# Where the scales of v are made: moving v's maxima, the store and load of its scales, and the first tile's attention-v inside a fused attention kernel

## The chip, the cores and the metric

The kernel runs on one core of a Trainium2 chip. The metric is the device time of one execution in microseconds (us); several executions are timed and their median is given. One further execution was taken with the hardware profiler, and all rows below come from it.

The engines are named as the profile names them: PE is TensorE's matmul side and PEld its weight load, DVE is VectorE, ACT is ScalarE, POOL is GpSimd, and SPq is SyncE's queue, from which this kernel issues every DMA.

## The reference, cut to what matters

```python
scores = scale * np.matmul(q, k.transpose(0, 1, 3, 2))      # 4 batches, 12 heads, 448 x 448
scores = np.einsum('bhij,hg->bgij', scores, w_pre)          # heads mixed
scores = scores - np.max(scores, axis=-1, keepdims=True)
attn = np.exp(scores)
attn = attn / (np.sum(attn, axis=-1, keepdims=True) + 1e-09)
attn = np.einsum('bhij,hg->bgij', attn, w_post)             # heads mixed again
attn_out = np.matmul(attn, v)
x = attn_out as [batch, 448, 768]
x = x + gated MLP of x (w_in, layer norm, token mixing w_sg, w_out)
x = two rotated token mixings and a channel matmul (w_theta, w_tok_r, w_tok_i, w_ch)
```

Only the attention part is touched by the change. It takes roughly the first 475 us of the span.

## The kernel before, in words

**Tiles and blocks.** The 448 query rows of a batch are cut into four tiles of 120, 120, 120 and 88 rows. Because heads are mixed, the scores of a tile (`s`, rows by heads by columns) are laid out again so that ten query rows times twelve heads fill 120 partitions: such a group of ten rows is a *block* (`blk`). A batch has 12 + 12 + 12 + 9 = 45 blocks, the last of a batch has only eight rows (96 partitions), and there are 180 blocks in all.

**Steps.** The function `attention` builds one long program: a loop over a step number s, from -7 to 191. In each step every engine gets its share for several blocks at different stages:

- SyncE: `relayout` of block s+7 (L217, a DMA from `s` to `blk`; five buffers, so block r waits until block r-5 has been used), and after it whatever the table `early` holds for the step
- TensorE: `premix` of block s+4 (L223, into `psB`, two buffers), matmuls for scores of a later tile (L203) and attention-v (L329) where the table `work` has them, then `postmix` of block s (L277, L278, L280)
- VectorE: `rowmax` of block s+4 (L229), `at_lo` of block s-1 (L308), the reciprocal for block s+2 (L250), `p_lo` of block s+1 (L262)
- ScalarE: the exponential of block s+3 (L236), `at_hi` of block s-1 (L302), copies of scores out of PSUM (L209, L207)
- GpSimd: `p_hi` of block s+2 (L255) and the small operation before the reciprocal (L244)
- after these, on whichever engine, what the table `late` holds for the step.

Each engine runs its own list in the order written. SyncE, too, issues its DMAs one after another: a DMA that has to wait holds all that are behind it. Since `premix` of block s+4 belongs to step s, the start of the `premix` of a block tells in which step TensorE is: block 44 is step 40. Its row is easy to find, since it alone in its batch has 96 partitions.

**The v path.** v is kept as two half-precision parts with a power-of-two scale per column. For a batch, three loads of v transposed (`vT`, L133, 448 KB each, two buffers) and three reductions (`v_max`, L148) give the maxima `vmx`. `v_scale` makes the scales `sv` and their inverses in six short VectorE operations (L87 to L156). `v_scale_out` (L162) stores the 768 scales to DRAM (`vs_d`), as 128 partitions of six single values. `v_scale_in` (L166) loads them back into all partitions (`vbc`); it waits until the store has ended. Then, for each of six pairs of heads, v is loaded (`vraw`, L173), multiplied (`v_mul`, GpSimd, L178), rounded (`v_hi`, ScalarE, L181) and its rest taken (`v_lo`, GpSimd, L185, three steps after `v_mul`).

**What sets the place of these.** The tables are filled by `put(table, step, function, arguments)`. `put_v(b, s, m, gap)` places `v_scale` of batch b late in step s, its store and load some steps after, and `v_mul` of the six pairs from step m on, `gap` steps apart. For the first batch it is called with steps of its own, for the other three with `first[b, 0] - VA[b]`, where `first[b, 0]` is the batch's first block (45, 90, 135). `DD[t][c]` says how many steps after the last block of tile t of any batch the attention-v of pair c is put.

Of the kernel before, what the change touches and what calls it, by code (L numbers as in the profile page):

```python
# [23 lines left out]
LD, LB, LE, LH, LL, EB, PB, SB = LDS  # L24
QO = 3
WARM = 16
VA = (0, 7, 7, 7)
VB = (0, 2, 3, 4)
XO = 1
DD = ((3, 5, 7, 9, 11, 13), (3, 4, 5, 6, 7, 8), (3, 4, 5, 6, 8, 10), (3, 4, 5, 6, 7, 8))  # L30
TX = 1
EX0 = 3
EX1 = 18
VM = 5
EXP_BITS = 0x7F800000


def attention(tc, nc, io, xT, B, extra, tail):
# [17 lines left out]
    with ExitStack() as es:  # L56
# [304 lines left out]
        early, work, late = {}, {}, {}  # L361

        def put(d, s, fn, *a):
            d.setdefault(s, []).append((fn, a))
# [6 lines left out]
        def unit(T, c):  # L371
            lo, hi = win[T]
            return lo + (c * (hi - lo)) // NP

        def put_v(b, s, m, gap):
            put(late, s, v_scale, b)
            put(early, s + 2, v_scale_out, b)
            put(early, s + 5, v_scale_in, b)
            for c in range(NP):
                put(early, m - 2, load_v, b, c)  # L380
                put(late, m, v_mul, b, c)
                put(late, m + 2, v_hi, b, c)
                put(late, m + 3, v_lo, b, c)
                m += gap

        for T in range(2, nt):
            b, t = tiles[T]
            for c in range(NP):
                put(work, unit(T, c), scores, b, t, c)
            put(early, win[T][0] - QO, load_q, b, t)  # L390
            if t == 0:
                for c in range(NP):
                    put(early, unit(T - 1, c), load_k, b, c)
                for c in range(0, NP, 2):
                    s = unit(T - 1, c)
                    put(early, s, load_vT, b, c)
                    put(late, s + 3, v_max, b, c)
                put_v(b, first[b, 0] - VA[b], first[b, 0] + VB[b], 3)
        for T in range(nt):
            b, t = tiles[T]  # L400
            l = last[tiles[T]]
            for c in range(NP):
                s = l + DD[t][c]
                put(work, s, attn_v, b, t, c)
# [26 lines left out]
            scores(0, 0, c)  # L431
        consts()
        for c in range(0, NP, 2):
            put(early, -LD + c // 2, load_vT, 0, c)
            put(late, -LD + 1 + c // 2, v_max, 0, c)
        put_v(0, -LD + 4, VM, 2)
        for s in range(-LD, NB + 12):
            if s == -LD:
                for fn, a in early.get(s - 1, []):
# [736 lines left out]
def build(tc, nc, io, out):  # L1176
    with tc.manual_schedule(), ExitStack() as top:
        dram = top.enter_context(tc.tile_pool(name="scratch", bufs=1, space=bass.MemoryType.DRAM))
        xT = dram.tile([DM, B * S], F32, name="xT")
        x2T = dram.tile([DM, B * S], F32, name="x2T")  # L1180
        d = Dense(tc, nc, io, xT, x2T, out)
        d.scratch(dram)
        right, left1, left2 = ExitStack(), ExitStack(), ExitStack()
        tail, win_es, last_u, end = moe1(d, left1, right)
        th_es = moe2(d, left2, win_es, last_u, left1)
        for i in range(4):
            tail.setdefault(-2 + 2 * i, []).append(d.step)
        jobs = d.decode_all(io["w_in"], HF, DFF, d.win_d)
        jobs += d.decode_all(io["w_in"], 0, HF, d.win_d, 128 * KE)
        attention(tc, nc, io, xT, B, jobs, tail)  # L1190
        while d.at < len(d.units):
            d.step()
        th_es.close()
        right.close()
        left2.close()
# [54 lines left out]
```

## Time and profile before

| | us |
|---|---|
| median of 3 runs | 1044.81 |
| lowest and highest | 1042.14 and 1047.06 |
| the profiled execution's own time | 1047.47 |
| span of the profiled execution | 1045.6 |
| PE busy, share of the span | 982.3, 94% |
| DVE, POOL, ACT busy | 775.5, 622.4, 586.6 |

The profiled execution lies 2.66 us above the median; 1.87 us of its time lie outside the span. A busy share is an average over the whole span and says nothing about one stage. What a stage is bound by is read from what ended the idle time of TensorE there, and from the chain of waits.

### The profile page before, as it was taken

How to read it: one execution, taken by the hardware profiler on the slowest of the kernel's cores; microseconds unless marked ns; L12 is line 12 of the kernel's file. 1: busy time of each engine (PE TensorE's matmuls, PEld its weight loads, DVE VectorE, ACT ScalarE, POOL GpSimd, SP SyncE). 2: the span in 40 equal slices, each digit the busy share in tenths (PEclk: the TensorE clock that was granted, in tenths of full speed). 3: DMA queues.
4: the chain of work that ended last, by engine and by line, in shares of the span. 5: the costliest groups of instructions: out<-in, count | busy, mean ns of one | idle time of the engine just before them, and what ended most of it. 6: DMA issues, size and time to landing. Idle time of an engine off the chain costs nothing.

```text
span 1045.6 us, 21830 instructions
## 1 busy us (share of the span) xinstructions
PE 982.3 (94%) x7848; PEld 742.7 (71%) x7848; DVE 775.5 (74%) x1458; ACT 586.6 (56%) x1374; POOL 622.4 (60%) x818
## 2 busy tenths in 40 slices
PE   7789999999999999997978999799999999999998
PEld 2445655565656555566756979587888999999997
DVE  2799878987888878985989998898896724925611
ACT  4577778786777778775754645454364412613310
POOL 0596558754686548854656877775666643753622
PEclk9899999999999999998989999999999999999999
DMA  5757565556556564347353676758956131130021
GB/s 191 154 167 221 142 139 183 180 168 129 161 193 203 131 158 152 131 108 265 113 155 89 213 225 199 229 188 274 335 184 226 41 106 31 32 106 16 31 76 53
DMA packets 135504, 159.47 MB, mean 153 GB/s; under 512 B 30309, under 2 KB 120933, under 8 KB 135397
## 3 DMA queue, kind: packets, MB, share of 16 engines
q1 hardware_dynamic: 135397, 158.08, 50.3%
q8 instruction: 63, 1.03, 0.4%
q14 instruction: 44, 0.36, 0.1%
HBM read 86.66 MB, written 32.85 MB: 114 GB/s over the span
## 4 chain that ended last, share of the span: by engine, by line
PE 57%; DVE 20%; DMA 9%; POOL 5%; issue 4%; ACT 3%; SPq 1%; DVEq 0%; ACTq 0%; POOLq 0%
PE ps L564 27%; PE psB L223 10%; PE psA L203 5%; PE psD L329 5%; DVE da L604 3%; PE psC L280 3%; PE psC L277 3%; DMA blk<-s 2%; PE psC L278 2%; DVE pl L262 2%; DVE da L602 2%; DVE dp L610 2%; DMA xres<-xT 2%; DVE dp L618 2%; DMA xraw<-xT 1%
## 5 line engine op out<-in xcount | busy, mean ns | idle before, releaser
L255 POOL TENSOR_SCALAR ph<-e,rc 120x448 f16<-120x448 f32 x180 | 163.9, 911 | 147.3 <-DVE rc L250 99.8
L223 PE MATMUL psB<-blk,kpre 120*120 120x448 f32 x360 | 177.3, 575 | 13.0 <-DMA blk<-s 8.2
L229 DVE TENSOR_REDUCE nmx<-psB 120x1 f32<-120x448 f32 x180 | 111.3, 618 | 49.9 <-PE psB L223 40.8
L262 DVE SCALAR_TENSOR_TENSOR pl<-e,rc,ph 120x448 f16<-120x448 f32 x180 | 147.4, 819 | 0.0
L236 ACT ACTIVATE e<-psB,nmx 120x448 f32<-120x448 f32 x180 | 114.3, 635 | 43.1 <-DVE nmx L229 43.0
L308 DVE SCALAR_TENSOR_TENSOR al<-psC,ah 128x480 f16<-128x480 f32 x180 | 116.1, 645 | 8.2 <-ACT ah L302 7.9
L277 PE MATMUL psC<-wh,ph 120*128 120x120 f16 x720 | 97.7, 218 | 10.9 <-DVE al L308 7.1
L302 ACT ACTIVATE ah<-psC 128x480 f16<-128x480 f32 x180 | 103.0, 572 | 7.6 <-PE psC L280 4.9
L209 ACT ACTIVATE s<-psA 120x896 f32<-120x896 f32 (+1 forms) x90 | 82.5, 917 | 42.5 <-PE psA L203 41.1
L564 PE MATMUL ps<-wtok,z 128*128 128x448 f32 x504 | 104.8, 368 | 0.4 <-POOL z L560 0.4
L564 PEld LDWEIGHTS ps<-wtok,z 128*128 128x128 f32 x504 | 94.4, 188 | 10.1 <-POOL z L560 0.8
L277 PEld LDWEIGHTS <-ph 120*128 120x128 f16 x720 | 68.8, 99 | 44.3 <-issue 18.6
L278 PE MATMUL psC<-wl,ph 120*128 120x120 f16 x720 | 97.1, 218 | 2.4 <-issue 2.4
L329 PEld LDWEIGHTS <-ah 128*128 128x128 f16 x1536 | 76.6, 99 | 31.2 <-issue 31.2
L203 PE MATMUL psA<-k,q 64*120 64x448 f32 (+1 forms) x384 | 96.2, 580 | 1.0 <-ACT s L209 1.0
L564 PE MATMUL ps<-wth,x2s 128*128 128x384 f32 x504 | 92.5, 338 | 2.0 <-POOL x2s L560 2.0
L564 PE MATMUL ps<-u,wch 128*128 128x448 f32 x432 | 89.9, 368 | 0.0
L564 PEld LDWEIGHTS ps<-wth,x2s 128*128 128x128 f32 x504 | 87.2, 188 | 2.8 <-POOL x2s L560 2.6
L560 POOL TENSOR_TENSOR z<-zz,z 128x384 fp32r<-128x384 f32 x56 | 61.9, 1125 | 45.8 <-ACT z L557 45.8
L564 PEld LDWEIGHTS ps<-u,wch 128*128 128x128 f32 x432 | 81.0, 188 | 8.1
L278 PEld LDWEIGHTS <-ph 120*128 120x128 f16 x720 | 71.2, 99 | 14.4 <-issue 14.2
L329 PE MATMUL psD<-vl,ah 128*128 128x64 f16 x768 | 78.0, 194 | 1.1 <-POOL vl L185 1.1
(124 smaller groups left out, 2171.9 us busy)
## 6 DMA issues: line engine op xcount, KB each, us to landing
blk<-s SPq DMA_DIRECT2D x176, 210.0 KB
draw<-in_w_in SPq DMA_DIRECT2D x24, 256.0 KB
vraw<-in_vN SPq DMA_DIRECT2D x24, 256.0 KB
k<-in_kvT SPq DMA_DIRECT2D x24, 224.0 KB
vT<-in_kvT SPq DMA_DIRECT2D x12, 448.0 KB
xraw<-xT SPq DMA_DIRECT2D x24, 224.0 KB
xres<-xT SPq DMA_DIRECT2D x24, 224.0 KB
x2T<-xres SPq DMA_DIRECT2D x24, 224.0 KB
```

Source lines behind the costliest of these rows:

```text
L203: nc.tensor.matmul(ps[e][:n, :S], q[p, o:o + n], k[p], start=True, stop=True)
L223: nc.tensor.matmul(ps[:r, :S], kpre[:r, :r], sblk.pop(s)[:r], start=True, stop=True)
L229: nc.vector.tensor_reduce(out=m[:r], in_=mix[s][:r, :S], axis=AX.X, op=ALU.max, negate=True)
L236: nc.scalar.activation(out=e[:r], in_=mix.pop(s)[:r, :S], func=AF.Exp, bias=nmx.pop(s)[:r], accum_out=sm[:r])
L255: nc.gpsimd.tensor_scalar(out=p[:r], in0=ex[s][0][:r], scalar1=rec[s][:r], scalar2=0.0, op0=ALU.mult, op1=ALU.add)
L262: nc.vector.scalar_tensor_tensor(out=p[:r], in0=ex.pop(s)[0][:r], scalar=rec.pop(s)[:r], in1=ph[s][:r], op0=ALU.mult, op1=ALU.subtract)
L277: nc.tensor.matmul(ps[:, jc, :, :n], cols(a, jc), wh[:r, :, :n], start=(jc == 0), stop=False)
L278: nc.tensor.matmul(ps[:, jc, :, :n], cols(a, jc), wl[:r, :, :n], start=False, stop=False)
L302: nc.scalar.activation(out=at_view(s, at[b, t][0]), in_=src, func=AF.Copy, scale=2.0 ** -17)
L308: nc.vector.scalar_tensor_tensor(out=al, in0=src, scalar=2.0 ** -17, in1=ah, op0=ALU.mult, op1=ALU.subtract)
L329: nc.tensor.matmul(ps[:, o:o + 64], a[:, i0:i0 + 128], v[:, jc, 64 * e:64 * e + 64], start=(o == 0 and m == 0), stop=(o == 320 and m == le ...
L564: self.nc.tensor.matmul(ps, l, r, start=(i == 0), stop=(i == len(terms) - 1))
```

## The change

It moves instructions; none is added or taken away. For the first batch the loads of `vT` move from steps -7, -6, -5 to steps -5, -4, -3, the three `v_max` from late in steps -6, -5, -4 to late in steps -2, -1, 0, `v_scale` from step -3 to step 1, and the first `v_mul` from step 5 to step 10 (two steps apart as before). For the other batches `v_scale` moves from seven to eleven blocks ahead of the batch. In all batches the store of the scales stands one step after `v_scale` instead of two, and their load eight steps after it instead of five, so that seven steps lie between store and load where there were three. `DD[0]` holds for the first tile of every batch: its attention-v moves from 3, 5, 7, 9, 11, 13 to 6, 7, 9, 10, 12, 13 steps after the tile's last block.

```diff
-VA = (0, 7, 7, 7)
+VA = (0, 11, 11, 11)
 VB = (0, 2, 3, 4)
-DD = ((3, 5, 7, 9, 11, 13), (3, 4, 5, 6, 7, 8), (3, 4, 5, 6, 8, 10), (3, 4, 5, 6, 7, 8))
+DD = ((6, 7, 9, 10, 12, 13), (3, 4, 5, 6, 7, 8), (3, 4, 5, 6, 8, 10), (3, 4, 5, 6, 7, 8))
-VM = 5
+VM = 10
...
         def put_v(b, s, m, gap):
             put(late, s, v_scale, b)
-            put(early, s + 2, v_scale_out, b)
-            put(early, s + 5, v_scale_in, b)
+            put(early, s + 1, v_scale_out, b)
+            put(early, s + 8, v_scale_in, b)
...
         for c in range(0, NP, 2):
-            put(early, -LD + c // 2, load_vT, 0, c)
-            put(late, -LD + 1 + c // 2, v_max, 0, c)
-        put_v(0, -LD + 4, VM, 2)
+            put(early, -LD + 2 + c // 2, load_vT, 0, c)
+            put(late, -2 + c // 2, v_max, 0, c)
+        put_v(0, 1, VM, 2)
```

SyncE at the start of the program, from the first block on (L217 is a block's relayout, L133 a load of v transposed, L162 the store of the scales, L166 their load). Before:

```order
L217 DMA blk<-s 120x1x448
L133 DMA vT<-in_kvT 128x2x448
L217 DMA blk<-s 120x1x448
L133 DMA vT<-in_kvT 128x2x448
L217 DMA blk<-s 120x1x448
L133 DMA vT<-in_kvT 128x2x448
L217 DMA blk<-s 120x1x448 x4
L162 DMA vs_d<-sv 128x6x1
L217 DMA blk<-s 120x1x448 x2
L588 DMA draw<-in_w_in 128x512
L217 DMA blk<-s 120x1x448
L166 DMA vbc<-vs_d 128x768
```

And now:

```order
L217 DMA blk<-s 120x1x448 x3
L133 DMA vT<-in_kvT 128x2x448
L217 DMA blk<-s 120x1x448
L133 DMA vT<-in_kvT 128x2x448
L217 DMA blk<-s 120x1x448
L133 DMA vT<-in_kvT 128x2x448
L217 DMA blk<-s 120x1x448 x4
L588 DMA draw<-in_w_in 128x512
L217 DMA blk<-s 120x1x448
L162 DMA vs_d<-sv 128x6x1
L217 DMA blk<-s 120x1x448 x2
L138 DMA q<-in_qT 128x720
```

The third load of v stood ahead of block 3 and stands ahead of block 5; the store stood ahead of block 7 and stands ahead of block 10.

SyncE ahead of the second batch (the row with 96 is block 44, the last of the first batch). Before:

```order
L217 DMA blk<-s 96x1x448
L138 DMA q<-in_qT 128x720
L217 DMA blk<-s 120x1x448 x3
L162 DMA vs_d<-sv 128x6x1
L217 DMA blk<-s 120x1x448 x2
L358 DMA xT<-x 128x3x120
```

And now:

```order
L358 DMA xT<-x 128x3x120
L217 DMA blk<-s 120x1x448 x2
L162 DMA vs_d<-sv 128x6x1
L588 DMA draw<-in_w_in 128x512
L217 DMA blk<-s 120x1x448
L217 DMA blk<-s 96x1x448
L138 DMA q<-in_qT 128x720
```

The store stood behind block 47 and ahead of block 48; it stands behind block 42 and ahead of block 43. In the third and fourth batch it moves in the same way, with no load of weights (`draw`) right behind it.

VectorE at the start, from its first reductions on (L148 is a maximum of v, L229 a row maximum, L87 the first operation of `v_scale`). Before:

```order
L148 TENSOR_REDUCE vmx<-vT 128x2 x2
L229 TENSOR_REDUCE nmx<-psB 120x1
L148 TENSOR_REDUCE vmx<-vT 128x2
L229 TENSOR_REDUCE nmx<-psB 120x1
L87 TENSOR_SCALAR vmx<-vmx 128x6
```

And now:

```order
L229 TENSOR_REDUCE nmx<-psB 120x1 x3
L250 RECIPROCAL rc<-rc 120x1
L148 TENSOR_REDUCE vmx<-vT 128x2
L229 TENSOR_REDUCE nmx<-psB 120x1
L250 RECIPROCAL rc<-rc 120x1
L262 SCALAR_TENSOR_TENSOR pl<-e,rc,ph 120x448
L148 TENSOR_REDUCE vmx<-vT 128x2
```

The first maximum of v stood ahead of the row maximum of block 0 and stands behind that of block 2.

## Rows read from the trace of the kernel before

**Rows 1.** The page: busy us, share of the span and instructions of each engine.

```profile
PE 982.3 (94%) x7848; PEld 742.7 (71%) x7848; DVE 775.5 (74%) x1458; ACT 586.6 (56%) x1374; POOL 622.4 (60%) x818
```

**Rows 2.** Chain of waits, first 200 us: start us, us, what the end waited on.

```profile
19.80 1.10 DVE vmx L148
20.91 3.46 DMA vT<-in_kvT
24.40 1.09 DVE vmx L148
...
27.23 11.20 DMA blk<-s
...
132.21 10.66 DMA blk<-s
```

**Rows 3.** Timeline of PE, premix of blocks 0, 5, 7, 10, 12, 43: [idle before <-releaser].

```profile
17.88 0.98 PE L223 MATMUL psB<-blk,kpre 120*120 120x448 f32 x2 [1.10 <-DMA blk<-s]
...
29.81 0.97 PE L223 MATMUL psB<-blk,kpre 120*120 120x448 f32 x2
...
38.57 1.82 PE L223 MATMUL psB<-blk,kpre 120*120 120x448 f32 x2 [5.38 <-DMA blk<-s]
...
45.83 0.97 PE L223 MATMUL psB<-blk,kpre 120*120 120x448 f32 x2
...
50.38 0.97 PE L223 MATMUL psB<-blk,kpre 120*120 120x448 f32 x2
...
128.82 0.97 PE L223 MATMUL psB<-blk,kpre 120*120 120x448 f32 x2
```

**Rows 4.** Timeline of SyncE's queue: the stores of the scales, and what followed.

```profile
26.74 0.38 SPq L162 DMA_DIRECT2D vs_d<-sv  x1
27.23 1.69 SPq L217 DMA_DIRECT2D blk<-s  x2
...
36.90 0.35 SPq L166 DMA_DIRECT2D vbc<-vs_d  x1
...
131.72 0.39 SPq L162 DMA_DIRECT2D vs_d<-sv  x1
...
363.53 0.39 SPq L162 DMA_DIRECT2D vs_d<-sv  x1
```

**Rows 5.** Timeline of DVE: row maxima of two neighbouring steps, and two p_lo.

```profile
30.91 0.62 DVE L229 TENSOR_REDUCE nmx<-psB 120x1 f32<-120x448 f32 x1
...
32.66 0.62 DVE L229 TENSOR_REDUCE nmx<-psB 120x1 f32<-120x448 f32 x1
...
119.97 0.67 DVE L262 SCALAR_TENSOR_TENSOR pl<-e,rc,ph 120x448 f16<-120x448 f32 x1
...
361.89 0.67 DVE L262 SCALAR_TENSOR_TENSOR pl<-e,rc,ph 120x448 f16<-120x448 f32 x1
```

**Rows 6.** Busy us by stretch: length, PE, PEld, DVE, ACT, POOL, PEclk, DMA share, GB/s.

```profile
140.00:150.00 10.00, 9.04 (x104) 5.08 (x104) 6.90 (x15) 6.30 (x16) 4.59 (x10) 1.00 0.81 200
190.00:200.00 10.00, 9.39 (x84) 5.56 (x85) 8.80 (x18) 7.15 (x19) 8.17 (x11) 0.83 0.44 145
250.00:260.00 10.00, 7.82 (x72) 3.93 (x70) 5.03 (x13) 5.43 (x15) 3.36 (x6) 1.00 0.58 84
370.00:380.00 10.00, 8.02 (x86) 4.52 (x84) 5.97 (x14) 5.80 (x14) 5.18 (x9) 1.00 0.56 135
```

**Rows 7.** The same in stretches of 2 us, the first and last with a lowered clock.

```profile
36.00:38.00 2.00, 0.00 (x0) 0.00 (x0) 0.00 (x0) 0.00 (x0) 0.00 (x0) 0.95 0.70 110
...
44.00:46.00 2.00, 2.00 (x19) 1.49 (x18) 1.86 (x6) 1.45 (x4) 1.23 (x2) 0.84 0.82 221
```

**Rows 8.** Timeline of PE: two more waits.

```profile
190.61 0.21 PE L277 MATMUL psC<-wh,ph 120*128 120x120 f16 x1 [2.05 <-DVE rc L250]
...
441.97 0.19 PE L329 MATMUL psD<-vl,ah 128*128 128x64 f16 x1 [1.06 <-POOL vl L185]
```

**Rows 9.** Chain of waits, 360 to 378 us: a piece in which PE waited for nothing shown.

```profile
371.40 1.64 issue
```

## The prediction

> **What bounds the kernel now.** I read the page's busy shares first: TensorE is busy for 94% of the span [rows 1], so nearly every idle stretch of TensorE inside attention is a loss, and what another engine saves is worth nothing unless TensorE was waiting for it. Then I read the chain of waits over the first 200 us [rows 2], which is where all first uses of the v path lie. It shows two kinds of loss. At the start VectorE reduces v before it may take row maxima: the chain runs through the maxima at 19.80 and 24.40 and through a load of v of 3.46 us between them. And twice it runs through a block's relayout that lasted 11.20 and 10.66 us. Then I read SyncE's timeline [rows 4]: both of these blocks were issued right behind a store of the scales (26.74 and 131.72). The store itself is small but slow: the load that waits for it follows at 36.90, 10.2 us after it. So a store of the scales holds up everything behind it in the DMA engines for some 11 us: a block issued behind it lands 11.7 us (27.23 + 11.20 - 26.74) or 11.15 us (132.21 + 10.66 - 131.72) after the store's issue. What that costs depends on one thing alone: how much work TensorE still has ahead when the store is issued.
>
> In the first batch it had too little: the premix of block 7 stood for 5.38 us [rows 3], and the granted clock fell to half (1.2 of 2.4 GHz), from 0.95 in 36 to 38 us to 0.84 in 44 to 46 us [rows 7], which is 0.2 us, three whole stretches and 0.64 us at half clock, 6.8 us in all. In the second batch TensorE's idle time in the ten microseconds of the landing is 0.96 us, in the third 2.18 us and in the fourth 1.98 us [rows 6], together 5.1 us. So in the later batches the store is nearly hidden now.
>
> **The change part by part.**
>
> *First batch, up to block 5.* Row maxima no longer stand behind the loads of v, so blocks 0 to 4 go through earlier. But the third load of v needs the buffer of the first, and so waits for the first maximum, which now stands behind the row maximum of block 2; on SyncE block 5 is queued behind that load, and TensorE waits for block 5. Following it by hand: the premix of block 0 starts at 17.88 and takes 0.98 [rows 3]; two more premixes and two groups of score matmuls of about that length bring block 2 to about 22.8, its row maximum to 23.4, the maximum of v (1.10 us [rows 2]) to 24.5; load and block are issued by 25.0. The load of v landed 3.46 us after its issue; I give block 5 that much at least, and a microsecond more for standing behind the load. So its premix starts at 28.5 to 29.5 instead of 29.81 [rows 3]. Nearly all of the gain ends in this new wait: 0.3 to 1.3 us are left.
>
> *First batch, the store.* v_scale now comes after p_lo of step 1 on VectorE. With the premix of block 5 (0.97) from 28.5 to 29.5 on, then its row maximum, at_lo, reciprocal and p_lo (a step takes VectorE 1.75 us, 32.66 - 30.91 [rows 5]) and the first operations of v_scale, about 1.0 us, the store goes out at 32.2 to 33.2, and block 10, right behind it, lands 11.7 us later, at 43.9 to 44.9; take 44.2. TensorE wants block 10 after three more steps of VectorE, at about 39. So the hole is there again, of some 5 us, and ends 1.6 us earlier than block 10 had its turn (45.83 [rows 3]). The half clock comes again too, but later: it lay on steps 3 to 5 (38.57 to 45.83, 7.3 us for what VectorE alone would allow in 5.3, a cost of 2.0), and now lies on steps 6 and 7, in the second of which scores of the third tile are worked as well. These two took 4.55 us (45.83 to 50.38 [rows 3]); they will take 6.55 (the same cost again) to 9.1 us (all of it doubled). Block 12 then has its turn at 50.75 to 53.3 instead of 50.38; without any half clock at 48.75 (44.2 + 4.55). I take **+1.0 us** (bounds -1.6 and +2.9), nearer to the same cost, since that is the measured one.
>
> *First batch, v itself.* The six v_mul, v_hi and v_lo move from steps 5 to 18 to steps 10 to 23, with nothing added; GpSimd and VectorE are as loaded during them as before, so I cost the move itself at nothing. But the attention-v of the last pair now stands in step 24, one step after its v_lo, where it stood six steps after. In the fourth batch two steps lie between them, and there TensorE waited 1.06 us for vl [rows 8]. With one step, the wait is at least that, and at most one step of about 2.5 us more, 3.5; or nothing, if TensorE is late for another reason. I take **+1.1 us** (0 to +3.5).
>
> *Batches two to four, the store.* This is the largest term. v_scale moves to step 34 of the batch before, and the store right behind it, with one block fewer ahead of it in the queue: block 43 (in the second batch) is now the first behind the store. When does the store go out? It follows the last p_lo ahead of it by 1.64 us (363.53 - 361.89 [rows 4, 5]); the p_lo of step 34 starts at 119.97 [rows 5], so the store would go out at 121.6. TensorE had its premix of block 43 at 128.82 [rows 3], 7.2 us later. Before, the store went out at 131.72 [rows 4], the block behind it landed 11.15 us later, and TensorE was idle for 0.96 us of it [rows 6]: the cover was 10.2 us, of steps that hold both scores and attention-v. Steps 35 to 38 hold less, so 7.2 us of cover stand against a landing after 11.15 to 11.7 us: TensorE stands for 4.0 to 4.5 us, 4.2 in the middle, in each of three batches, 12.6 us. In the second a load of weights of 256 KB lies in between as well, which can add up to 1.5 us. The idle time of now, 5.1 us, goes with the store that caused it. Net **+7.5 us** (+4 to +11).
>
> *The clock after these holes.* The hole of 2.05 us at 190.61 [rows 8] was followed by a mean clock of 0.83 over ten microseconds [rows 6], 3.4 us at half; that of 5.38 us by 6.8 us at half. Half of that time is lost where TensorE is the bound: 1.7 to 3.4 us a hole, 2.5 for one of about 4 us. The broken-up idle times of the third and fourth batch left the clock at 1.00 [rows 6]. I take one such fall, **+2.5 us** (0 to +9 for none to three).
>
> *SyncE and the load of the scales.* SyncE no longer stands at L166 until 36.90; with seven steps between, the store has ended. That wait was hidden behind the late blocks already, so I cost it at nothing; were it not hidden, the gain would be the second rival's. The attention-v of the later batches' first tiles keeps its distance to v_lo; spreading it over lighter steps can give up to 1 us a batch, or take as much; nothing in the sum.
>
> **Sum.** +1.0 + 1.1 + 7.5 + 2.5 = +12.1 us. On the profiled execution's own time that is 1047.47 + 12.1 = 1059.6; that execution lies 2.66 us above the median, so on the median 1044.81 + 12.1 = **1056.9, say 1057 us**.
>
> **The rivals.**
>
> *The later holes are covered.* If blocks land as soon as the store has ended, 10.2 us after its issue, and TensorE reaches block 43 later than it did, by one light step (1.5 us), each hole is 1.5 us, as large as now, and the clock stays up. Then about +1 is left: 1046 us. For it: VectorE has 26% of its time free and might make the scales earlier. Against it: VectorE reaches v_scale only with p_lo, and both measured landings were over 11 us.
>
> *Faster: the holes come from SyncE standing at the load of the scales, not from the blocks behind the store.* SyncE did stand there until 36.90, with block 10 behind it, and the change takes that away. Then the hole of the first batch (5.38) and its half clock (half of 6.8) go, and the 5.1 us of the later ones: -13.9 + 1.1, 1032 us. It decides as soon as a block behind the store lands within the 7.2 us of cover. Against it: block 7 was issued at 27.23, before SyncE stood, and its landing is what the chain names.
>
> *The fetch gaps stay.* In the fourth batch TensorE stopped in the middle of its matmuls for 1.64 us for nothing the trace names [rows 9], 7.9 us behind the store (371.40 - 363.53); I counted these idle times as the store's. If they are not, 4.2 us of the 5.1 (third and fourth batch) stay: +4.2, 1061 us. The Trainium skill speaks for this ("DMA: Bandwidth & Descriptors", Queues, rings and completion order): an engine takes turns between the rows of queues packet by packet, so a stream of instructions on a queue of its own would not stand behind the store. By that rule the time would be this rival's; the place of the gap, behind a store, speaks against it.
>
> **How the numbers follow.** Forecast (holes move and grow) 0.56; fetch gaps stay, or the clock falls three times, 0.10; covered 0.24; faster 0.10. The range has to hold the covered case and the upper bounds of the forecast: its terms span from about +2 to +26, rarely all at one end; I give 1043 to 1068. A measurement of this kernel tells a change of about 0.5% (5.2 us) from none. Slower by more than that: 0.66, the first two cases; within: 0.23; faster: 0.11.
>
> **What would show it.** Right: the store about 121.6 us into the span, block 43 the one that TensorE waits for, for about 4 us, and the like twice more; block 5 behind the third load of v; a hole of 5 us at block 10 ending near 44; no wait at L166. Wrong: blocks behind a store landing in under 8 us, or no idle time of TensorE over 2 us at blocks 43, 88 and 133; or the premix of block 5 before 28; for the clock, rows at 1.00 after all holes.

## The result and the profile after

The changed kernel takes 1060.32 us (median of 6 runs, 1058.94 to 1063.51), the kernel before 1045.53 us beside it (6 runs, 1042.14 to 1047.74): a ratio of 1.0145, with a 95% interval of 1.0123 to 1.0167. The change costs 14.8 us. The profiled execution after took 1063.51 us, the longest of the six, and its span is 1061.7 us. Of all the executions below, two ran in a slow state with a far lower granted clock (1550.73 us in experiment 7 and 1090.39 us in experiment 10) and are in no ratio.

The busy times of the page, after (engine, busy us, share of the span, instructions):

```profile
PE 987.4 (93%) x7848; PEld 747.1 (70%) x7848; DVE 773.4 (73%) x1458; ACT 586.7 (55%) x1374; POOL 621.8 (59%) x818
```

Against [rows 1] the work is the same, and the span is 16.1 us longer. So the engines do nothing more; TensorE stands, and it runs slower behind the stands.

SyncE's timeline after, the first store of the scales and its surroundings, and the stores of the later batches (start, us, operation; they answer to [rows 4]):

```profile
22.99 0.38 SPq L133 DMA_DIRECT2D vT<-in_kvT  x1
23.47 3.63 SPq L217 DMA_DIRECT2D blk<-s  x4
27.15 0.77 SPq L588 DMA_DIRECT2D draw<-in_w_in  x1
28.03 0.82 SPq L217 DMA_DIRECT2D blk<-s  x1
31.27 0.38 SPq L162 DMA_DIRECT2D vs_d<-sv  x1
...
123.49 0.37 SPq L162 DMA_DIRECT2D vs_d<-sv  x1
...
244.64 0.37 SPq L162 DMA_DIRECT2D vs_d<-sv  x1
...
364.18 0.37 SPq L162 DMA_DIRECT2D vs_d<-sv  x1
```

TensorE's timeline after, the premixes of blocks 0, 5, 9 and 10, and of blocks 43, 88 and 133 (start, us, operation, in brackets the idle time ahead and what ended it; they answer to [rows 3]):

```profile
16.36 0.98 PE L223 MATMUL psB<-blk,kpre 120*120 120x448 f32 x2 [0.82 <-DMA blk<-s]
27.44 0.98 PE L223 MATMUL psB<-blk,kpre 120*120 120x448 f32 x2 [1.85 <-DMA blk<-s]
41.51 1.82 PE L223 MATMUL psB<-blk,kpre 120*120 120x448 f32 x2 [6.05 <-DMA blk<-s]
44.33 1.56 PE L223 MATMUL psB<-blk,kpre 120*120 120x448 f32 x2
...
134.93 1.85 PE L223 MATMUL psB<-blk,kpre 120*120 120x448 f32 x2 [4.07 <-ACT e L236]
...
255.66 0.98 PE L223 MATMUL psB<-blk,kpre 120*120 120x448 f32 x2 [3.65 <-issue]
...
376.46 1.68 PE L223 MATMUL psB<-blk,kpre 120*120 120x448 f32 x2 [4.91 <-issue]
```

There are the wait for the third load of v at block 5, a hole of 6 us in the first batch, and one of about 4 us 11 to 12 us behind each later store (134.93 - 123.49 = 11.4, 255.66 - 244.64 = 11.0, 376.46 - 364.18 = 12.3). In all three TensorE runs out of work 7.4 us behind the store (the premix less its idle time, less the store's issue). The first of these is named ACT. The chain of waits says why (start, us, what); `draw` is the load of weights that stands right behind this store, ScalarE works through its list in order, and the exponential that frees a `psB` buffer stands behind the copy of `draw`:

```profile
123.92 9.58 DMA draw<-in_w_in
133.52 0.05 ACT dp L599
...
133.85 0.42 ACT dl L600
134.27 0.62 ACT e L236 x2
```

All three later holes lowered the clock. Windows after (us, busy time of each engine, granted TensorE clock, DMA share, GB/s); the stretches behind blocks 43, 88 and 133:

```profile
134.00:136.00 2.00, 1.07 (x2) 0.63 (x3) 1.86 (x5) 1.96 (x6) 0.00 (x0) 0.57 0.58 160
136.00:138.00 2.00, 2.00 (x28) 1.43 (x26) 2.00 (x8) 1.31 (x5) 1.23 (x2) 0.50 0.63 230
138.00:140.00 2.00, 2.00 (x16) 1.40 (x13) 0.99 (x4) 0.86 (x3) 1.36 (x2) 0.50 0.44 166
140.00:142.00 2.00, 2.00 (x11) 0.60 (x10) 1.15 (x3) 0.04 (x1) 0.00 (x0) 0.73 0.00 0
...
256.00:258.00 2.00, 2.00 (x35) 1.61 (x33) 1.31 (x4) 0.00 (x0) 0.00 (x0) 0.79 0.55 181
258.00:260.00 2.00, 2.00 (x9) 0.74 (x6) 0.53 (x1) 0.00 (x0) 1.11 (x2) 0.50 0.67 238
260.00:262.00 2.00, 2.00 (x30) 1.23 (x30) 0.32 (x2) 0.82 (x3) 0.00 (x0) 0.86 0.53 185
...
376.00:378.00 2.00, 1.54 (x3) 0.55 (x4) 0.00 (x0) 0.57 (x1) 0.00 (x0) 0.65 0.64 224
378.00:380.00 2.00, 2.00 (x33) 2.00 (x32) 1.82 (x4) 0.72 (x2) 0.40 (x1) 0.50 0.65 201
```

A mean of 0.57 over 2 us means 1.7 us at half clock, and so on: 6.8, 3.4 and 3.4 us (of the third, the last stretch, at 0.99, is left out), of which half is lost, 6.8 us in all. A fourth new fall lies behind the wait at block 5, with means of 0.61 and 0.53 from 28 to 32 us: 3.4 us at half clock.

The other new wait is at the attention-v of the first tile, where the last parts of v come late (TensorE's timeline after):

```profile
83.27 0.19 PE L329 MATMUL psD<-vl,ah 128*128 128x64 f16 x1 [0.45 <-POOL vl L185]
93.61 0.21 PE L329 MATMUL psD<-vl,ah 128*128 128x64 f16 x1 [2.42 <-POOL vl L185]
```

**Where the time went.** Setting each block's premix after against the same block's before gives the cost by place (start after minus start before, us):

| block | 0 | 5 | 12 | 24 | 30 | 42 | 45 | 75 | 91 | 92 | 134 | 137 | 165 |
|---|---|---|---|---|---|---|---|---|---|---|---|---|---|
| shift | -1.5 | -2.4 | -1.5 | -4.7 | +1.9 | +1.9 | +9.0 | +7.2 | +13.0 | +9.9 | +16.6 | +14.3 | +14.3 |

The steps up are the holes and the half clock behind them; the steps down (1.1 us at block 48, 3.1 at 92, 2.3 at 137) are the smaller waits of the kernel before, which lay at those places and are gone. Net: the first batch +1.9, the second +5.3 (6.0 up to block 48, less 0.7 by block 75: the fall of the clock behind the wait of 2.05 us [rows 8] did not come again), the third +2.75, the fourth +4.4. The start of -1.5 at block 0 varies from execution to execution: in six kernels with v's maxima in their old place block 0 came at 16.5 to 17.9 us, in eight with the moved ones at 16.1 to 17.4, and [rows 3] happen to show the latest. From block 165 to the end of the span it took 599.6 us before and 601.3 after. All fourteen kernels traced here are the same from there on, and it took them 596.7 to 601.3, so that last +1.8 is not counted as a cost of the change.

### The profile page after: what moved, and what is told of

It is laid out like the page before. It is cut to its first block, busy times and chain, and to the rows that moved or that the text cites. A ratio compares the mean times of both kernels' runs of the same rounds, so it can differ in the third digit from the quotient of the medians.

```text
span 1061.7 us, 21828 instructions
## 1 busy us (share of the span) xinstructions
PE 987.4 (93%) x7848; PEld 747.1 (70%) x7848; DVE 773.4 (73%) x1458; ACT 586.7 (55%) x1374; POOL 621.8 (59%) x818
## 4 chain that ended last, share of the span: by engine, by line
PE 59%; DVE 16%; DMA 8%; POOL 7%; issue 5%; ACT 4%; SPq 1%; POOLq 0%; DVEq 0%; ACTq 0%
PE ps L564 30%; PE psB L223 9%; PE psA L203 5%; PE psD L329 5%; DMA blk<-s 3%; PE psC L280 3%; PE psC L277 2%; DVE da L604 2%; PE psC L278 2%; POOL vraw L178 2%; DVE da L602 2%; POOL ph L255 2%; DMA xraw<-xT 2%; DVE dp L618 1%; DVE dp L610 1%
## 5 line engine op out<-in xcount | busy, mean ns | idle before, releaser
L223 PE MATMUL psB<-blk,kpre 120*120 120x448 f32 x360 | 180.5, 584 | 23.8 <-DMA blk<-s 9.7
L229 DVE TENSOR_REDUCE nmx<-psB 120x1 f32<-120x448 f32 x180 | 111.1, 617 | 64.7 <-PE psB L223 64.1
L277 PE MATMUL psC<-wh,ph 120*128 120x120 f16 x720 | 99.0, 220 | 10.7 <-DVE al L308 7.9
```

The source lines that it names most:

```text
L223: nc.tensor.matmul(ps[:r, :S], kpre[:r, :r], sblk.pop(s)[:r], start=True, stop=True)
L229: nc.vector.tensor_reduce(out=m[:r], in_=mix[s][:r, :S], axis=AX.X, op=ALU.max, negate=True)
L277: nc.tensor.matmul(ps[:, jc, :, :n], cols(a, jc), wh[:r, :, :n], start=(jc == 0), stop=False)
```

## Experiments

All times are medians; a ratio is to the kernel before, run beside it on the same chip.

**1 and 2. Which batches?** One kernel has the change without the later batches' part, the other has that part alone. The first, against the changed kernel:

```diff
-VA = (0, 11, 11, 11)
+VA = (0, 7, 7, 7)
...
-            put(early, s + 1, v_scale_out, b)
-            put(early, s + 8, v_scale_in, b)
+            put(early, s + (2 if b else 1), v_scale_out, b)
+            put(early, s + (5 if b else 8), v_scale_in, b)
```

> The changed kernel with the second to fourth batch's scales made, stored and loaded where they were before; the first batch and the attention-v of the first tiles stay as changed. Store theory (the cost comes from stores of the scales issued with too little work ahead of TensorE in the later batches): block 42 comes about 2 us later than before, no hole of over 2 us at blocks 43, 88 and 133, so 1046 to 1049 us. Rival (the moved attention-v of the first tiles, or the moved v work of the first batch, is what costs): stays within 4 us of the changed kernel, 1056 to 1062 us.

Measured: 1045.97 us, ratio 1.0026 (1.0005 to 1.0046), so +2.7 us. The second, against the kernel before:

```diff
-VA = (0, 7, 7, 7)
+VA = (0, 11, 11, 11)
...
-            put(early, s + 2, v_scale_out, b)
-            put(early, s + 5, v_scale_in, b)
+            put(early, s + (1 if b else 2), v_scale_out, b)
+            put(early, s + (8 if b else 5), v_scale_in, b)
```

> The kernel before with the scales of the second to fourth batch alone made, stored and loaded at the places of the changed kernel. Store theory: holes of 3.5 to 5 us at blocks 43, 88 and 133 and half clock behind them, +12.5 us by the blocks' shifts in the changed kernel's trace (6.0 - 0.7 + 2.75 + 4.4), 1058 us. Rival (the first batch or the first tiles' attention-v costs): 1045 to 1049 us. If this run and the run with the old later batches do not add up to the change's +14.8 within 3 us, the two parts act on each other.

Measured: 1058.13 us, ratio 1.0148 (1.0116 to 1.0181), so +15.4 us. TensorE's timeline of this kernel at blocks 43, 88 and 133:

```profile
133.71 1.01 PE L223 MATMUL psB<-blk,kpre 120*120 120x448 f32 x2 [3.65 <-ACT e L236]
...
252.62 0.98 PE L223 MATMUL psB<-blk,kpre 120*120 120x448 f32 x2 [2.54 <-DMA blk<-s]
...
373.00 1.29 PE L223 MATMUL psB<-blk,kpre 120*120 120x448 f32 x2 [4.37 <-DMA blk<-s]
```

The store theory holds: the three holes are in this kernel and not in the other. Here the trace names the block's landing at blocks 88 and 133, where the changed kernel's trace named nothing ("issue"), so these are the same holes. The parts add up to 18.1 against 14.8 us, 3.3 apart, just past the 3 us set beforehand; with intervals of 2 to 3.5 us on each side that is no sign of parts that act on each other.

**3 and 4. Is it the store's many small writes?** Each partition's six scales are stored side by side, in both kernels.

```diff
-                nc.sync.dma_start(out=vs_d[b].rearrange("(c p) -> p c", p=128), in_=raws.pop(("sv", b)))
+                nc.sync.dma_start(out=vs_d[b].rearrange("(p c) -> p c", p=128), in_=raws.pop(("sv", b)))
...
-            raw, sc = raws["v", b, c], vsb[b][:, 128 * c:128 * c + 128]
+            raw, sc = raws["v", b, c], vsb[b].rearrange("q (p c) -> q c p", c=NP)[:, c]
```

> The changed kernel with the 768 scales stored as 128 runs of 24 bytes (each partition's six values side by side) instead of 768 single values; the load stays one contiguous broadcast and v_mul reads the scales six apart. Every place in the order stays. Store theory (it is the many small writes that hold what stands behind): the store ends in 2 to 3 us, holes at blocks 9, 43, 88 and 133 and their half clock go, 19.6 us in the later batches and about 4 in the first: 1036 us (1032 to 1043). Rival, SyncE standing at the load: it does not stand in the changed kernel, so 1060 us. Rival, the gaps of the third and fourth batch are fetches of instructions that have nothing to do with the store: these two stay, 5.8 and 6.7 us, so about 1049 us. Unknown: what v_mul on GpSimd takes with scales six apart; if twice as long, TensorE may wait for vl in every batch.

> The kernel before with the 768 scales stored as 128 runs of 24 bytes instead of 768 single values, everything else in its place. Store theory: the wait at block 7 (5.38 us), its half clock (half of 6.8) and the 5.1 us of idle time in the later batches go, -13.9 us at most: 1032 us (1031 to 1040). Rival, SyncE standing at the load: the same time here, since the load no longer waits either. Rival, fetches that have nothing to do with the store: 4.2 us less of a gain, 1036 us at best.

Measured: the changed kernel comes to 1041.46 us, ratio 0.9981 (0.9966 to 0.9996), some 17 us less by the ratios than with single values; the kernel before to 1038.70 us, ratio 0.9970 (0.9954 to 0.9985). In neither trace does TensorE wait inside attention for anything that the trace leaves unnamed, and the holes at blocks 43, 88 and 133 are gone. So are the gaps in the middle of matmuls of the kernel before [rows 9]: from block 90 to 92 and from 135 to 137 it is 3.1 and 2.3 us faster than before. SyncE standing at the load falls as an explanation for the changed kernel, where it does not stand there either way, and so do gaps that have nothing to do with the store.

The gain is 5 to 7 us short of what I had expected of the two. In the first batch VectorE becomes the bound. Windows of the kernel before with the new store (PE, PEld, DVE, ACT, POOL busy):

```profile
36.00:38.00 2.00, 1.02 (x8) 0.32 (x8) 2.00 (x5) 0.88 (x3) 0.63 (x3) 1.00 0.82 223
38.00:40.00 2.00, 1.80 (x19) 0.95 (x17) 2.00 (x6) 1.53 (x5) 1.28 (x3) 1.00 0.88 236
40.00:42.00 2.00, 2.00 (x15) 0.83 (x12) 2.00 (x6) 1.10 (x4) 1.84 (x3) 1.00 0.67 198
```

The third busy time is VectorE's: it is busy for all of these 6 us, and TensorE for 4.82. The reading of scales six apart made `v_mul` on GpSimd slower, from 1650 to 1907 ns in the changed kernel (medians of 24), and that is hidden. The Trainium skill gives this direction for kernels of GpSimd's own cores ("GPSIMD Engine Reference", Performance pitfalls for Q7 kernels: half as much again for reads with a step of over 8 bytes); with a step of 24 bytes it is 16% here.

**5. The wait for vl.** The changed kernel with the first batch's v work two steps earlier.

```diff
-VM = 10
+VM = 8
...
-            put(early, s + 8, v_scale_in, b)
+            put(early, s + (8 if b else 6), v_scale_in, b)
```

> The changed kernel with the first batch's six v_mul (and what follows them) two steps earlier, from step 8, and the load of its scales in step 7 instead of 9; everything else as changed. Wait theory: the loss of 6.6 us between blocks 24 and 30 of the changed kernel (from -4.7 to +1.9 us against the kernel before) comes from the last v_lo standing one step ahead of its attention-v; with three steps between, the waits for vl (2.42 and 0.45 us) and the half clock behind them go: 3 to 5 us less, 1055.5 to 1057.5 us, and no row with POOL vl in the first batch. Rival: the loss is attention-v that only moved from earlier steps to these (the moved places of the first tile), so the waits go or move to VectorE but the time stays: within 1.5 us of the changed kernel, 1059 to 1062 us.

Measured: 1054.27 us, ratio 1.0111 (1.0091 to 1.0131), against 1.0145 that is 3.5 us less. No wait for vl is left in the first batch, and between blocks 26 and 30 this kernel gains 4.0 us on the changed one; the clock, which in the changed kernel was 0.83, 0.50 and 0.82 in the three stretches from 92 us on, is 1.00 here. The wait theory holds.

**6. The moved attention-v alone,** in the kernel before.

```diff
-DD = ((3, 5, 7, 9, 11, 13), (3, 4, 5, 6, 7, 8), (3, 4, 5, 6, 8, 10), (3, 4, 5, 6, 7, 8))
+DD = ((6, 7, 9, 10, 12, 13), (3, 4, 5, 6, 7, 8), (3, 4, 5, 6, 8, 10), (3, 4, 5, 6, 7, 8))
```

> The kernel before with only the attention-v of the first tiles moved (6, 7, 9, 10, 12, 13 steps after the tile's last block instead of 3, 5, 7, 9, 11, 13). Wait theory: v's parts are ready six steps ahead, so nothing waits, and work that moves three steps later moves no time: 1043 to 1047 us, blocks 15 to 24 earlier and blocks from 30 on level. Rival: the denser steps themselves cost, in the first and in the later batches: 3 us or more over the kernel before.

Measured: 1043.99 us, ratio 1.0012 (0.9996 to 1.0028): no difference that can be told.

**7. SyncE at the load of the scales.** The kernel before with the load alone moved back.

```diff
-            put(early, s + 5, v_scale_in, b)
+            put(early, s + 7, v_scale_in, b)
```

> The kernel before with only the load of the scales later, five steps behind the store instead of three, so that SyncE no longer stands at it; the store stays where it was. Store theory: the blocks behind the store land as late as before, so the hole at block 7 (5.38 us), the idle times of the later batches and the time stay: 1042 to 1047 us. Rival, SyncE standing at the load is what makes the holes: they go, 9 to 14 us less than before, 1031 to 1036 us.

Measured: 1044.47 us, ratio 1.0013 (1.0001 to 1.0026). The hole has not moved. TensorE's timeline of this kernel at block 7, the store's own time in its chain, and SyncE's wait for the store (us in total, times, longest):

```profile
38.78 1.82 PE L223 MATMUL psB<-blk,kpre 120*120 120x448 f32 x2 [4.41 <-DMA blk<-s]
```

```profile
27.35 10.99 DMA vs_d<-sv
```

```profile
SPq L138 <- DMA vs_d<-sv: 3.5, 1, 3.5
```

SyncE's stand is not wholly gone in the first batch: it waits 3.5 us for the store, until 38.36, where it stood 6.5 us before, and the load goes out at 38.77. But blocks 7 to 11 are all issued ahead of this wait (27.84 to 33.46), where blocks 10 and 11 stood behind it before, and block 7 lands as late as it did. In the later batches, where SyncE stood 1.8 to 2.2 us at the load before, it no longer stands there, and the time is the same. The rival falls.

**8. Half of the single values.** The changed kernel with three of the six pairs stored as single values and three as runs of 12 bytes.

```diff
-                nc.sync.dma_start(out=vs_d[b].rearrange("(c p) -> p c", p=128), in_=raws.pop(("sv", b)))
+                sv = raws.pop(("sv", b))
+                h = DM // 2
+                nc.sync.dma_start(out=vs_d[b, :h].rearrange("(c p) -> p c", p=128), in_=sv[:, :3])
+                nc.sync.dma_start(out=vs_d[b, h:].rearrange("(p c) -> p c", p=128), in_=sv[:, 3:])
```

> The changed kernel with half of the scales (three pairs) stored as 384 single values and the other half as 128 runs of 12 bytes, in two stores right behind each other; places as changed. Cover theory: the stores end after about half of the 10 us, so the block behind them lands within the 7.2 us that TensorE has ahead at blocks 43, 88 and 133: holes there of under 1 us and no half clock, in the first batch a hole at blocks 9 or 10 of under 2 us: 15 to 20 us less than the changed kernel, 1040 to 1046 us. Rival, any store of single values holds the queue as long, whatever their number: holes of 3.5 to 5 us stay, 1057 to 1062 us.

Measured: 1056.39 us, ratio 1.0122 (1.0106 to 1.0139). The cover theory was wrong here: the hole at block 133 is still 3.52 us, and the block that ends it has its turn 10.9 us behind the first store (371.25 - 360.36), against 12.3 with all 768. Half of the values, with the runs of 12 bytes behind them, do not take half of the time.

**9. What the store's time hangs on.** A probe on the kernel before, with the load right behind the store (each store below is followed by the load of what it wrote) and another way to store in each batch.

```diff
-            put(early, s + 2, v_scale_out, b)
-            put(early, s + 5, v_scale_in, b)
+            put(early, s + 2, v_scale_in, b)
...
+            if b == 0:
+                nc.sync.dma_start(out=vs_d[b].rearrange("(c p) -> p c", p=128), in_=sv)
...
+            elif b == 1:
+                nc.sync.dma_start(out=vs_d[b, :h].rearrange("(c p) -> p c", p=128), in_=sv[:, :3])
+                nc.sync.dma_start(out=bc[:, :h], in_=vs_d[b, :h].partition_broadcast(128))
+                nc.sync.dma_start(out=vs_d[b, h:].rearrange("(p c) -> p c", p=128), in_=sv[:, 3:])
...
+            elif b == 3:
+                for u in range(2):
+                    nc.sync.dma_start(out=vs_d[b].rearrange("(p a u) -> p a u", p=128, u=2)[:, :, u],
+                                      in_=sv[:, 3 * u:3 * u + 3])
...
+            else:
+                nc.sync.dma_start(out=vs_d[b].rearrange("(p c) -> p c", p=128), in_=sv)
```

> A probe on the kernel before: the load of the scales stands right behind their store in every batch, so that SyncE waits there until the store has ended, and each batch stores in another way. Batch 1: 768 single values, neighbours in DRAM coming from 128 different partitions (as before). Batch 2: first 384 single values in that way, their load, then 128 runs of 12 bytes, their load. Batch 3: 128 runs of 24 bytes. Batch 4: 768 single values in two stores, each partition's six within its own 24 bytes of DRAM. What is read is the time from a store's issue to the issue of the load behind it. Count theory (each single write costs the same, 10.2 us / 768): batch 2 gives 5.1 us and about 2.5 us, batch 3 under 3 us, batch 4 about 10 us. Place theory (what costs is that different partitions write neighbouring values): batch 4 as fast as batch 3, 2 to 4 us, and batch 2 9 us and 2.5 us. The run with half of the single values, where the block behind landed 10.8 us after the first store, speaks against the count theory unless the runs of 12 bytes take 5 us themselves.

It was executed once, and its time (1056.41 us) says nothing here. SyncE's timeline of the probe, stores (`vs_d`) and the loads behind them (`vbc`):

```profile
26.25 0.38 SPq L167 DMA_DIRECT2D vs_d<-sv  x1
36.01 0.34 SPq L168 DMA_DIRECT2D vbc<-vs_d  x1
...
134.24 0.39 SPq L171 DMA_DIRECT2D vs_d<-sv  x1
143.61 0.33 SPq L172 DMA_DIRECT2D vbc<-vs_d  x1
143.99 0.42 SPq L173 DMA_DIRECT2D vs_d<-sv  x1
147.89 0.32 SPq L174 DMA_DIRECT2D vbc<-vs_d  x1
...
258.69 0.34 SPq L184 DMA_DIRECT2D vs_d<-sv  x1
260.16 0.33 SPq L185 DMA_DIRECT2D vbc<-vs_d  x1
...
373.80 2.07 SPq L179 DMA_DIRECT2D vs_d<-sv  x2
382.62 0.34 SPq L181 DMA_DIRECT2D vbc<-vs_d  x1
```

From a store's issue to the load behind it: 9.8 us for 768 single values, 9.4 for 384, 3.9 for runs of 12 bytes (with the load of 143.61 still ahead of them), 1.5 for runs of 24 bytes, 8.8 for 768 single values of which each partition writes its own 24 bytes. Each of these is a single store. Both theories fall: neither the count nor the neighbourhood in DRAM sets the time. A store of single values takes 9 to 10 us here, a store of runs does not. Nor are the DMA engines busy with the values for that long. Windows of the probe behind the first store, the last two figures being the busy share of the DMA engines and GB/s:

```profile
32.00:34.00 2.00, 2.00 (x25) 1.30 (x22) 2.00 (x5) 1.19 (x3) 0.74 (x1) 1.00 0.00 0
34.00:36.00 2.00, 0.18 (x4) 0.02 (x1) 1.49 (x4) 1.19 (x3) 1.36 (x3) 1.00 0.00 0
```

By the packet records of the trace the last of the 4-byte packets starts at 27.7 us, and the store counts as ended only at 36.0, after some 8 us in which the engines move next to nothing. What it waits for there no row tells; why is open.

**10. The store on another queue.** The changed kernel with the store issued by ScalarE.

```diff
-                nc.sync.dma_start(out=vs_d[b].rearrange("(c p) -> p c", p=128), in_=raws.pop(("sv", b)))
+                nc.scalar.dma_start(out=vs_d[b].rearrange("(c p) -> p c", p=128), in_=raws.pop(("sv", b)))
```

> The changed kernel with the store of the scales issued by ScalarE instead of SyncE, so that it stands on another queue than the blocks; values, places and sizes as changed. Theory 1, the store's writes hold the DMA engines themselves whatever queue they come by (or what they write to): holes of 3.5 to 5 us at blocks 43, 88 and 133 stay, 1056 to 1062 us. Theory 2, the blocks stand behind the store in SyncE's own queue alone and the engines take turns between queues: the holes shrink to under 1.5 us, 1041 to 1047 us.

Measured: 1048.42 us, ratio 1.0045 (1.0028 to 1.0063), 10 us less than the changed kernel by the ratios. The profiled execution, at 1043.79 us, was the fastest of its ten, so its trace shows the mechanism better than the size. The holes are gone in it: the premixes of blocks 43, 88 and 133 start at 125.70, 242.93 and 357.62, with 1.01 us of waiting at most. SyncE's and ScalarE's DMAs around the second store:

```profile
115.64 2.75 SPq L217 DMA_DIRECT2D blk<-s  x2
118.02 0.37 ACTq L162 DMA_DIRECT2D vs_d<-sv  x1
```

These two rows say why the holes are gone, and it is neither theory. The two blocks are 43 and 44, and they go out ahead of the store. In the changed kernel SyncE waited at the store for VectorE's scales (3.0 to 3.6 us in the later batches), with block 43 behind it; now ScalarE waits there, and SyncE goes on. The later stores, at 234.07 and 349.94, find blocks 88 and 133 already issued, at 231.24 and 347.26. So the run shows what it is worth to let these blocks go 2.4 to 2.8 us ahead of the store, and cannot tell whether a block issued behind the store would pass it on another queue.

What SyncE did issue behind the store speaks against it. In the chain of waits, loads that it issued 0.4, 1.3 and 0.4 us behind the three later stores:

```profile
118.45 11.77 DMA q<-in_qT
...
235.35 11.41 DMA draw<-in_w_in
...
350.37 13.12 DMA q<-in_qT
```

By the packet records the loads of `q` right behind the three later stores had their last packet 11.2, 11.2 and 12.4 us after their issue; in the second kernel of experiments 3 and 4, with the quick store, the same three loads need 5.8, 6.1 and 6.9 us. So the store delays transfers of another queue too. The Trainium skill states a rule ("DMA: Bandwidth & Descriptors", Queues, rings and completion order: an engine takes turns between rows of queues); no row of this run shows a transfer that passes the store by it.

**11 and 12. A kernel that beats both.** The kernel before with runs of 24 bytes and the first batch's maxima of v behind the row maxima; then the same with three buffers for v transposed. The first, against the kernel of experiment 4:

```diff
-            put(early, s + 2, v_scale_out, b)
-            put(early, s + 5, v_scale_in, b)
+            put(early, s + (2 if b else 1), v_scale_out, b)
+            put(early, s + (5 if b else 4), v_scale_in, b)
...
-            put(early, -LD + c // 2, load_vT, 0, c)
-            put(late, -LD + 1 + c // 2, v_max, 0, c)
-        put_v(0, -LD + 4, VM, 2)
+            put(early, -LD + 2 + c // 2, load_vT, 0, c)
+            put(late, -2 + c // 2, v_max, 0, c)
+        put_v(0, 1, VM + 1, 2)
```

> The kernel before with the scales stored as 128 runs of 24 bytes and, in the first batch alone, the maxima of v moved behind the first row maxima as in the changed kernel, the store one and the load four steps behind v_scale, and v_mul from step 6 on instead of 5; attention-v and the later batches as before. Store theory: the store no longer holds blocks, so the maxima moved back cost nothing at the store and give the first five blocks their earlier place; but VectorE, which is busy all the time in blocks 5 to 13, and the wait for the third load of v take most of it back: 0 to 3 us less than the kernel before with the runs of 24 bytes, 1036 to 1039 us. Rival: the third load of v still holds block 5 and no more than the start moves: the same time as that kernel, 1038.7, within 1 us; slower than it by over 1 us if the later v work meets attention-v.

The second, against the first:

```diff
-        vT_p = pool_r("a_vT", 2)
+        vT_p = pool_r("a_vT", 3)
```

> The kernel with runs of 24 bytes and the first batch's maxima moved back, with three buffers for v transposed instead of two, so that its third load no longer waits for the first maximum. By the prediction's step on block 5 its wait of 1.96 us and the half clock behind it go, so block 5 starts at about 25.7 us. Theory 1, what the wait took is on the path: 1.5 to 3 us less than with two buffers, 1035.5 to 1037 us. Theory 2, VectorE is the bound from block 5 to 13: block 12 comes at most 1 us earlier, 1037.5 to 1039 us.

Measured: 1038.31 us, ratio 0.9959 (0.9943 to 0.9975), and 1037.90 us, ratio 0.9944 (0.9931 to 0.9958). Both beat the kernel before; between themselves and against the runs of 24 bytes alone (0.9970) the intervals overlap, so only the store's gain is shown. TensorE's timeline at the wait in question, first with two buffers (block 5), then with three (block 4):

```profile
27.62 0.98 PE L223 MATMUL psB<-blk,kpre 120*120 120x448 f32 x2 [1.96 <-DMA blk<-s]
```

```profile
25.32 1.43 PE L223 MATMUL psB<-blk,kpre 120*120 120x448 f32 x2 [1.96 <-DMA blk<-s]
27.74 1.67 PE L223 MATMUL psB<-blk,kpre 120*120 120x448 f32 x2
```

The third load no longer waits for a buffer, and the wait of 1.96 us only moves one block ahead: block 4, issued behind the second load and ahead of the third, now lands late, and block 5 starts 0.1 us later than with two buffers.

## Why the prediction was right, and where its steps were off

**The mechanism and the total held.** 1057 us were forecast, 1060.3 came, by the mechanism named: the later stores have too little work of TensorE ahead of them. As a difference, +12.1 us were forecast and +14.8 measured. The total is closer than its terms, since the wait for vl and the clock cost more than the sum had and the first store and the net of the later ones less; that part is luck. The parts:

- *Up to block 5:* right in kind. A gain of 0.3 to 1.3 us was forecast; measured from block 0 on it is 0.9 us (11.93 us from block 0 to block 5 before, 11.08 after). Block 5 itself came at 27.44, under the 28 us that the prediction gave as a sign of being wrong, because block 0 came 1.5 us early. The kernel before happens to show the least here: the six traces with the maxima in their old place need 11.9 to 15.3 us, the eight with the moved ones 11.0 to 11.2, so by most of these traces the gain is larger than forecast. The half clock behind the new wait, 3.4 us, was not in the sum. The reason given, the third load waiting for a buffer, is not needed for the wait: experiment 12 takes that away, and TensorE stands as long one block earlier.
- *The first store:* a hole of 5 us at block 10 that ends near 44 was forecast. The hole is 6.05 us, at block 9, and block 10 had its turn at 44.33. Block 9 was issued 3.2 us ahead of the store (28.03 against 31.27), directly behind 256 KB of weights: the step that failed is "the block behind the store is the first that is late". That step does not fail each time: with the same order in this place the late block is block 9 in the first kernel of experiments 1 and 2, by 5.76 us, and block 10 in experiment 5, by 4.42 us, with block 9 in time. Block 12 came 1.5 us early instead of 1.0 late; with the early start taken off it is level, inside the bounds of -1.6 and +2.9. The half clock began within the hole (means of 0.67, 0.50, 0.50 and 0.62 from 38 to 46 us), not on the steps behind it.
- *vl:* mis-sized. +1.1 was taken (0 to 3.5); the waits are 2.87 us, and the longer one lowered the clock, 3.4 us at half, which the sum did not have. Experiment 5 gives 3.5 us for both.
- *The later holes:* 12.6 us were forecast, 4.07 + 3.65 + 4.91 = 12.6 us measured. TensorE's work behind the store was taken as 7.2 us and was 7.4 in all three. The equality of the sums is better than the working: the second batch's hole ended through the load of weights and ScalarE. The block itself was hardly earlier, though: the trace records its landing up to 134.11, 0.8 us ahead of ScalarE's release at 134.89, so the weights made at most 0.8 us of this hole. What goes in exchange is 6.5 us by the blocks' shifts (1.1 + 3.1 + 2.3) instead of 5.1.
- *The clock:* the term that was mis-sized most. One fall at +2.5 was taken, three came, 6.8 us, within the bounds of 0 to 9. The working took [rows 6] as a sign that idle times of about 2 us leave the clock up; single holes of 3.65 to 4.91 us did not, nor did the waits of 1.85 and 2.42 us.
- *SyncE at L166 and the moved attention-v,* at nothing: experiments 7 and 6 agree; in the changed kernel SyncE does not wait at L166 in any batch.

**The rivals.** The covered holes did not come: the blocks had their turn 11.0 to 12.3 us behind the store's issue. SyncE's stand as the cause fell in experiments 7 and 3. The fetch gaps that stay fell too: the idle times of [rows 9] are gone from their places after the change and with a quick store. That rival rests on a queue of its own not standing behind the store, and the runs show otherwise. What SyncE issued behind ScalarE's store was late (experiment 10). And loads of instructions, of 16 KB on queue 8 of the page, whose packets take 1.0 us in the median and at most 1.8 us away from the stores, took up to 5.9 us in the first nine microseconds behind a store of single values (3.8 us in the kernel before, at 135.10) and at most 1.5 us behind a store of runs. So the prediction's sentence that a store "holds up everything behind it in the DMA engines" stands as far as the runs reach. That the gaps of [rows 9], in the middle of matmuls that wait for no block, are such late loads of instructions is not shown; with the store on ScalarE's queue two gaps of 0.73 and 0.68 us are left 9.7 and 10.7 us behind the fourth store.

## What to carry to other kernels

Ask of each small DMA not how many bytes it moves but how long it takes and what is issued behind it, on its own queue or another; here 3 KB in single values held blocks of 210 KB for 11 us, and writing each partition's values side by side was worth more than any place in the order that was tried. Where such a store must stay, let what TensorE needs next go out ahead of it, which another engine's issuing it brought here (experiment 10), or count TensorE's work from the store's issue to the first thing issued behind it, weights that another engine takes in order included. A hole of 4 us cost about 6.5 us here ((12.6 + 6.8) / 3), since each brought a half clock behind it.

## What the runs showed of the hardware that was not expected

- 384 single values took 9.4 us to store and 768 took 9.8, 128 runs of 24 bytes 1.5; for some 8 of the 9.8 us the DMA engines moved next to nothing (experiment 9).
- The same store on ScalarE's queue delayed loads on SyncE's: those issued 0.4 to 1.3 us behind it took 11.4 to 13.1 us (experiment 10).
- A block can be late by a store that was issued 3.2 us behind it: block 9 landed 13.4 us after its issue in the changed kernel, and in another kernel with the same order it was in time.
